# Seven-product downs two steps earlier in an attention and mixture-of-experts kernel, with weight forms, loads and attention pieces moved

## The chip, the cores and the metric

The kernel runs on one core of a Trainium2 chip. The metric is device time in microseconds: the median of the runs of one kernel. The kernel before takes 505.33 us (7 runs, 505.01 to 506.3). The engines are TensorE (PE; its weight loads are listed apart as PEld), VectorE (DVE), ScalarE (ACT), GpSimd (POOL) and SyncE (SP). Each runs its own list of instructions in order; what one needs from another it waits for.

## The reference

```python
def _attn_ref(q, k, v):                       # q, k, v: 8 x 8 x 576 x 64
    k_p = k.reshape(B, H, Sp, pool, D).mean(axis=3)      # pool = 8, Sp = 72
    v_p = v.reshape(B, H, Sp, pool, D).mean(axis=3)
    scores = scale * np.matmul(q, k_p.transpose(0, 1, 3, 2))
    scores = scores - np.max(scores, axis=-1, keepdims=True)
    attn = np.exp(scores)
    attn = attn / (np.sum(attn, axis=-1, keepdims=True) + 1e-09)
    return np.matmul(attn, v_p)

def _moe_ref(x, domain_probs, w1, w2):        # x: 4608 x 512, E = 4, F = 1024
    p = domain_probs / (domain_probs.sum(-1, keepdims=True) + 1e-09)
    for e in range(E):
        h = np.maximum(x @ w1[e], 0.0)
        out += p[:, e:e + 1] * (h @ w2[e])
```

x is the attention's output, its heads side by side, token by token.

## The kernel before

**Chunks and steps.** The 4608 tokens are nine chunks of 512: chunk c below 8 holds the first 512 tokens of batch c, and chunk 8 holds the 64 left-over tokens ("rem") of all eight batches. A step is one pair (chunk c, expert e), numbered s = 4c + e; the loop of L983 runs through them. In step s PE makes the hidden values of (c, e), the "up", and multiplies those of step s - 1 with w2, the "down", so the two are interleaved. Most matmuls take weights of w1 or hidden values as stationary operand.

**Ups.** An up is a product of two-by-two blocks. `up_plain` (L671) makes it with eight block products (32 matmuls of 512 columns). `up_seven` (L731) makes it with seven products (`product`, L654; eight matmuls of 256 columns for each, half of them in each half j of the step), which need sums and differences of blocks: the weight forms S1, S2, S4, S3 of w1 (`combine_w1`, L608) and the forms of x (`forms_of`, L619). Each product's bank in PSUM is copied by ACT (`keep`, L702), added to another one with the ReLU by DVE (`relu_sum`, L707), or put through a ReLU by ACT (L711).

**Downs.** A plain down (`down`, L861) is 32 matmuls of 512 columns, and `merge` adds each result, times its probability, to an accumulator. A seven-product down (`half_of`, L770, and `up_down`, L789) uses seven half products of 256 columns, four matmuls each, twice in a step. It needs forms of the hidden values (`sums_of`, L718: three DVE instructions and a GpSimd one, L728) and of w2 (`combine_w2`, L640: t1, t2, t4 go to w2_t, and the last overwrites a block of w2_bf, so that it must come after the last plain down with that expert). `splits` (L715) says which steps have such a down. Its results are merged by four DVE adds for each half of the step (L766); for expert 0 two of them are a scaling by DVE (L821) and one by ACT.

**What sets the order.** All engines' lists are written out by hand. `point()` and `slot()` (L972 to L981) count places; `placed` names what is emitted at a place, and `slot()` first takes one entry of `forms_due`. A step has 16 places, 8 of them slots. `second_attention` (L530) puts the attention of batch 1 at places 42 to 71, and `attention(c)` (L551) that of batch c + 1 at places 2n + 1 after the start of chunk c, for n of its table, while chunk c's experts run. The pieces: a fold adds the eight rows of a pooled key or value (DVE L198 to L249 for batch 1, L214 to L222 for batch 2, POOL for keys from batch 3); `second_keys` and `second_queries` transpose on PE, `keys` and `queries` by DMA (SP); `scores` runs four matmuls and ACT's exp; `context` multiplies with the values and divides on DVE (L385, L386); `turn` transposes x by DMA (L417). The rem pieces of two batches come in odd chunks (L560 to L564).

**Queues.** Loads are DMAs issued by GpSimd (L950 to L965 for the first ones), in the order w1(1), w1(2), w2(1), w1(3), k1, w2(2), q1, v1, w2(3). They stand in its one list with its arithmetic, so a load that waits for its buffer holds up the sums behind it. `loads_wait` (L243) is a copy of one element by which GpSimd waits for kpT before it issues the next loads. w2_t of experts 2 and 3 is also the home of the raw values of batches 1 and 2. SP issues the transposes by DMA and the stores.

**Which forms where.** Before: w1(0) and w2(0) without their last forms, and w1(2), in step 1; w1(3) in step 2; w1(1) and x of chunk 1 in step 4; w1(0)'s last and w2(2) in step 5; w2(3) in step 6; w2(1) in steps 7 and 8 and w2(0)'s last in step 8, all on DVE. Step 4 starts with the eight pieces of the plain down of (0, 3); the plain up of (1, 0) follows (L1051 to L1055).

Of the kernel before, what the change touches and what calls it, by code (L numbers as in the profile page):

```python
# [18 lines left out]
def kernel(  # L19
# [99 lines left out]
    def load_first_q(half):  # L119
# [5 lines left out]
        )  # L125

    def load_q_rem(b):
        if b % 2 == 0:
            q_rems[b // 2] = qpool.tile([P, H, D], BF16, name="q_rem", bufs=2)
        lo = (b % 2) * REM  # L130
        nc.gpsimd.dma_start(
            out=q_rems[b // 2][lo:lo + REM],
            in_=q[b, :, NT:S, :].rearrange("h p d -> p h d"),
        )
# [107 lines left out]

    def loads_wait(b):  # L243
        nc.gpsimd.tensor_copy(out=mark[:], in_=state[("kpT", b)][0:1, 0, 0:1])

# [284 lines left out]
    def second_attention():  # L530

        lo, hi = halves

        return {
            42: [lambda: fold_keys(1, lo)],
            44: [lambda: fold_keys(1, hi), lambda: load_k(2)],
            48: [second_keys],
            51: [lambda: second_queries(0)],
            52: [lambda: second_queries(1), lambda: load_q(2), lambda: load_q_rem(2)],
            54: [lambda: scores(1, 0)],  # L540
            56: [lambda: scores(1, 1), lambda: fold_values(1, lo)],
            58: [lambda: scores(1, 2), lambda: fold_values(1, hi)],
            60: [lambda: scores(1, 3)],
            61: [lambda: context(1, 0), lambda: turn(1, 0)],
            63: [lambda: context(1, 1), lambda: turn(1, 1)],
            66: [lambda: context(1, 2), lambda: turn(1, 2)],
            69: [lambda: context(1, 3), lambda: turn(1, 3)],
            71: [lambda: load_v(2)],
        }

    def attention(c):  # L551
# [8 lines left out]
        if c % 2:  # L560
            i = c // 2
            q_at = 15 if b < B else 2
            for n, piece in zip((0, 8, 11, 12), (rem_queries, rem_scores, rem_context, rem_turn)):
                add(q_at + n, lambda piece=piece: piece(i))  # L564
# [5 lines left out]
        if c == 1:  # L570
            add(3, lambda: queries(b))
            add(2, *key_parts(b)[:2])
            add(3, *key_parts(b)[2:])
            add(3, lambda: keys(b), lambda: loads_wait(b))
            add(3, lambda: (load_q(b + 1), load_q_rem(b + 1)))
            for pair in range(NPAIR):
                add(8 + pair, lambda pair=pair: scores(b, pair))
            for n, part in enumerate(value_parts(b)):
                add(7 + n, part)
            mixed = (12, 13, 14, 15)  # L580
        else:
# [8 lines left out]
        if more:  # L590
            add(4, lambda: load_half(b + 1, k, "kraw", 0))
            add(11, lambda: queries(b + 1))
            add(8, lambda: load_half(b + 1, k, "kraw", 1))
            add(16, *key_parts(b + 1))
            add(21, lambda: load_half(b + 1, v, "vraw", 0))
            add(27, lambda: load_half(b + 1, v, "vraw", 1))
            add(24, lambda: keys(b + 1))
# [117 lines left out]
    def splits(c, e):  # L715
        return (1, 2) <= (c, e) < (B, E - 1)

# [212 lines left out]
    with tc.manual_schedule(engines={ENG.PE, ENG.DVE, ENG.Activation, ENG.Pool, ENG.SP}):  # L930
# [25 lines left out]
        load_w1(2)  # L956
        load_w2(1)
        load_w1(3)
        load_k(1)
        load_w2(2)  # L960
        load_q(1)
        load_v(1)
# [20 lines left out]
        for s in range(len(steps) + 1):  # L983
# [15 lines left out]

            nothing = [lambda: None] * 4  # L1000
            if s == 1:
                w, u, x = combine_w2(0), combine_w1(0), forms_of(0)
                forms_due.extend([lambda w=w, u=u, n=n: (w[n](), u[n]()) for n in range(3)])
                forms_due.extend(nothing[:1] + combine_w1(2))
                for part in x[:3]:
                    part()
            elif s == 2:
                x[3]()
                forms_due.extend(nothing + combine_w1(3))
            elif s == 4:  # L1010
                x = forms_of(1)
                u1 = combine_w1(1)
                forms_due.extend(nothing + [
                    lambda: (u1[0](), u1[1]()), lambda: (u1[2](), u1[3]()), lambda: x[0](),
                    lambda: (x[1](), x[2]()),
                ])
            elif s == 5:
                x[3]()
                forms_due.extend(u[3:] + nothing[:2] + combine_w2(2))
            elif s == 6:  # L1020
                v3 = combine_w2(3)
                forms_due.extend(nothing[:1] + v3[:1] + nothing[:2] + v3[1:])
            elif s == 7:
                v2 = combine_w2(1)
                forms_due.extend(nothing[:1] + v2[:1] + nothing[:3] + v2[1:2])
            elif s == 8:
                forms_due.extend(nothing[:1] + w[3:] + v2[2:3] + nothing[:2] + v2[3:])
            elif s == E * B + 1:
                reload_w2(E - 1)
            for j in range(2):  # L1030
# [20 lines left out]
                elif s == E:  # L1051
                    for n in range(4):
                        between(j, n)
                    if j:
                        up_plain(c, e, range(FCH))  # L1055
                elif splits(*steps[s - 1]):
                    up_down(c, e, j, *steps[s - 1])
# [32 lines left out]
```

## Time and profile before

| what | us |
|---|---|
| median of the runs | 505.33 |
| the profiled execution, its own time | 505.47 |
| its span, first to last instruction | 503.8 |
| PE busy | 492.5 |
| DVE busy | 354.7 |
| ACT busy | 287.1 |
| POOL busy | 182.4 |

The profile is of one execution. A busy time is the union of an engine's instructions; the span is 1.67 us shorter than the time of the execution. A row of the timeline gives the start, the length, engine, line, operation, what is written and read, how many instructions are merged in it, and in brackets how long the engine sat idle before it and what ended that. Where this text says "from start to start", the gap is counted from one matmul's start to the next, less the usual distance, since a matmul's recorded end overlaps with the next one. A few matmuls are missing from the records. By that count PE lost 9.8 us against full streaming between 17 and 142 us, and 12.7 us in all of the rest up to 500 us, where nearly all of it is the usual distance of 0.109 us between matmuls of 256 columns against 0.107 us of streaming.

### The profile page before, as it was taken

Reading aid. Unit: us, or ns where it says so; the run is one execution under the profiler, and the core shown is the slowest. Engines: PE = TensorE matmul, PEld = TensorE weight load, DVE = VectorE, ACT = ScalarE, POOL = GpSimd, SP = SyncE. Lnnn points to the kernel's source line nnn. Section 1 sums busy time; section 2 is a strip of 40 time slices with the busy share of each in tenths; the row PEclk is TensorE's granted clock in tenths of the full one; section 3 lists DMA queues with packets and bytes.
Section 4 is the critical chain, followed back from the end, with each engine's and each line's share of the span. In section 5 each row is a group of like instructions: output and inputs, shape, how many; then the busy total and the mean of one; then the engine's idle time right before and its main releaser. Section 6 shows DMA issues by size and latency. Waiting matters only on the chain.

```text
span 503.8 us, 10971 instructions
## 1 busy us (share of the span) xinstructions
PE 492.5 (98%) x4485; PEld 392.5 (78%) x4499; DVE 354.7 (70%) x643; ACT 287.1 (57%) x531; POOL 182.4 (36%) x169
## 2 busy tenths in 40 slices
PE   8899899999999999999999999999999999999996
PEld 3746554667788888888788888888888888888884
DVE  1364889667877767777777777767777767776674
ACT  3654444645576567655766576666665565556650
POOL 8463202145423662266126722661115111512110
PEclk9999999999999999999999999999999999999999
DMA  9999999963826364935573286332210110012003
GB/s 123 205 205 205 202 170 175 124 62 47 98 83 98 48 66 113 109 48 60 111 108 59 19 128 110 53 44 60 64 20 13 44 43 12 1 44 64 2 1 83
DMA packets 84754, 41.90 MB, mean 83 GB/s; under 512 B 48720, under 2 KB 80208, under 8 KB 84704
## 3 DMA queue, kind: packets, MB, share of 16 engines
q0 software_dynamic: 43200, 22.91, 35.7%
q1 hardware_dynamic: 41104, 17.77, 17.1%
q8 instruction: 35, 0.57, 0.5%
q10 hardware_dynamic: 400, 0.52, 0.3%
q14 instruction: 15, 0.12, 0.1%
HBM read 45.69 MB, written 9.44 MB: 109 GB/s over the span
## 4 chain that ended last, share of the span: by engine, by line
PE 82%; DMA 9%; DVE 4%; POOL 2%; issue 1%; ACT 1%; POOLq 0%; ACTq 0%
PE g_ps L660 36%; PE u_ps L782 34%; PE o_ps L876 5%; DMA w_bf<-in_moe_w_dram 5%; DMA q_sb<-in_q_dram 3%; PE two L272 2%; PE two L395 1%; PE h_ps L678 1%; DMA H_sb<-in_v_dram 1%; DVE acc L766 1%; DVE H_sb L708 1%; POOL w_bf L146 1%; DVE x_tok L386 1%; DVE w_bf L651 0%; PE o_ps L891 0%
## 5 line engine op out<-in xcount | busy, mean ns | idle before, releaser
L660 PEld LDWEIGHTS <-w_bf 128*128 128x128 bf16 x1848 | 177.8, 98 | 29.3 <-issue 3.2
L766 DVE SCALAR_TENSOR_TENSOR acc<-u_ps,p_all,acc 128x512 f32<-128x512 f32 (+1 forms) x204 | 121.1, 594 | 76.7 <-ACT u_ps L819 72.4
L728 POOL TENSOR_TENSOR h_s<-H_sb,h_s 128x1024 bf16<-128x1024 bf16 x29 | 61.4, 2117 | 232.1 <-DVE h_s L727 232.1
L660 PE MATMUL g_ps<-xT,w_bf 128*128 128x256 bf16 x928 | 129.9, 273 | 0.5 <-DVE H_sb L708 0.5
L660 PE MATMUL g_ps<-xf,w_bf 128*128 128x256 bf16 x792 | 109.8, 272 | 0.7 <-ACT g_ps L803 0.4
L704 ACT COPY r<-g_ps 128x512 f32<-128x512 f32 x140 | 82.0, 586 | 49.8 <-PE g_ps L660 45.2
L708 DVE CUSTOM_DVE_ANT_0 H_sb<-g_ps,r 128x512 bf16<-128x512 f32 x140 | 96.2, 688 | 13.2 <-ACT r L704 8.8
L782 PEld LDWEIGHTS <-H_sb 128*128 128x128 bf16 x928 | 86.7, 98 | 18.2 <-DVE H_sb L726 4.9
L782 PE MATMUL u_ps<-w_bf,H_sb 128*128 128x256 bf16 x696 | 95.3, 273 | 0.4 <-DVE H_sb L726 0.3
L711 ACT ACTIVATE H_sb<-g_ps 128x512 bf16<-128x512 f32 x124 | 74.0, 597 | 20.5 <-PE g_ps L660 20.5
L782 PEld LDWEIGHTS <-h_s 128*128 128x128 bf16 x696 | 68.1, 98 | 7.9
L803 ACT COPY g_ps<-g_ps 128x512 f32<-128x512 f32 x58 | 33.1, 570 | 65.3 <-PE g_ps L660 65.3
L782 PE MATMUL u_ps<-w_t,h_s 128*128 128x256 bf16 x464 | 69.6, 273 | 0.0
L876 PE MATMUL o_ps<-w_bf,H_sb 128*128 128x512 bf16 x205 | 51.3, 379 | 0.7 <-issue 0.2
L819 ACT COPY u_ps<-u_ps 128x256 f32<-128x256 f32 x58 | 20.7, 357 | 32.9 <-PE u_ps L782 32.6
L782 PE MATMUL u_ps<-w_t,H_sb 128*128 128x256 bf16 x232 | 35.0, 273 | 0.0
L782 PE MATMUL u_ps<-w_bf,h_s 128*128 128x256 bf16 x232 | 34.8, 273 | 0.0
L876 PEld LDWEIGHTS <-H_sb 128*128 128x128 bf16 x216 | 20.6, 98 | 18.2 <-issue 0.8
L276 ACT ACTIVATE expT<-two 72x1024 bf16<-72x1024 f32 x28 | 28.5, 1017 | 1.3 <-PE two L272 1.3
L386 DVE TENSOR_TENSOR x_tok<-two,inv 128x512 bf16<-128x512 f32 x32 | 22.1, 691 | 1.1
L821 DVE TENSOR_SCALAR acc<-u_ps,p_all 128x512 f32<-128x512 f32 x14 | 10.5, 750 | 16.5 <-ACT u_ps L819 16.5
L807 ACT COPY u_ps<-u_ps 128x256 f32<-128x256 f32 x58 | 21.1, 363 | 0.0
(119 smaller groups left out, 435.1 us busy)
## 6 DMA issues: line engine op xcount, KB each, us to landing
out_dram<-acc SPq DMA_DIRECT2D x32, 256.0 KB, 2.4
w_bf<-in_moe_w_dram POOLq DMA_DIRECT2D x17, 256.0 KB, 8.9
w_bf<-in_moe_w_dram POOLq DMA_DIRECT2D x8, 512.0 KB, 14.8
q_sb<-in_q_dram POOLq DMA_DIRECT2D x7, 512.0 KB, 10.3
raw_kv<-in_k_dram POOLq DMA_DIRECT2D x10, 288.0 KB, 6.5
raw_kv<-in_v_dram POOLq DMA_DIRECT2D x10, 288.0 KB, 6.1
raw_kv<-in_k_dram POOLq DMA_DIRECT2D x2, 576.0 KB, 15.6
w_t<-in_v_dram POOLq DMA_DIRECT2D x2, 576.0 KB, 13.7
```

The lines of the kernel that those rows point to most:

```text
L276: nc.scalar.activation(out=state[("expT", b)][:, 2 * pair:2 * pair + 2].rearrange("j h r s p -> j s (h r) p"), in_=two[0:SP].rearrange("j ...
L386: nc.vector.tensor_tensor(out=x_tok, in0=c_ps[:, :, :, 0:D], in1=inv[:].unsqueeze(3).to_broadcast([P, 2, NPAIR, D]), op=ALU.mult,)
L660: nc.tensor.matmul(bank[:, t, :], lhsT=w1_bf[:, e, block, kc, lo:lo + P], rhs=x[:, kc, :], start=(first and t == 0 and kc == 0), stop=(t = ...
L704: nc.scalar.copy(out=r[:], in_=ps[:])
L708: nc.vector._custom_dve(TENSOR_ADD_SAT, out=out, in0=ps[:], in1=r[:], s0=BIG, s1=0.0)
L711: nc.scalar.activation(out=out, in_=ps[:], func=ACT.Relu)
L728: lambda: nc.gpsimd.tensor_sub(out=s4, in0=a12, in1=s2),
L766: nc.vector.scalar_tensor_tensor(out=acc, in0=ps, scalar=prob, in1=acc, op0=ALU.mult, op1=ALU.add,)
L782: nc.tensor.matmul(out, lhsT=lhs[0][:, lhs[1] + f, lhs[2]], rhs=rhs[0][:, rhs[1] + f, rhs[2]], start=(start and f == 0), stop=(f == FCH // ...
L803: nc.scalar.copy(out=s[:], in_=g[:])
L807: nc.scalar.copy(out=two[:, lo], in_=one[:, lo])
L876: nc.tensor.matmul(sums[r][:], lhsT=hidden[(c, e)][:, fc, r * P:(r + 1) * P], rhs=w2_bf[:, e, fc, :], start=(fc == 0), stop=(fc == FCH - 1),)
```

## The change

- `splits` begins at (1, 0) instead of (1, 2): the downs of these two steps are made with seven products. The plain up of (1, 0) is followed by the sums of its hidden values.
- The forms they need come earlier: w2(0)'s last in step 1; w1(1)'s in step 2; w2(1)'s all on GpSimd, placed at 60 in step 3, behind a one-element copy that waits for the values of batch 1 and the load of v2 (both from place 71). w1(3)'s are split over the end of step 2 and the start of step 3; w2(2)'s and w2(3)'s go to steps 5 to 8.
- k1 is loaded ahead of w1(3), and q1 in two halves by heads. The folds and transposes of k1 move up by one place, two contexts of batch 1 move back by one.
- The attention of batch 2 in chunk 1 is moved back and spread: queries from n = 3 to 4, folds from 2 and 3 to 6 and 7, keys from 3 to 7, the mark and loads behind it to 8, scores from 8 to 11 to 8, 10, 12, 14, values from 7 to 9, contexts from 12 to 15 to 16, 18, 20, 21; the halves of k3 from 4 and 8 to 8 and 12.
- The rem pieces stand at 0, 9, 13, 14 instead of 0, 8, 11, 12 after their start; in the last chunk they start at 3 instead of 2.

```diff
+    def load_q_halves(b):
+        raws[("q", b)] = qpool.tile([P, H, NR, D], BF16, name="q_sb")
+        for hs in halves:
+            nc.gpsimd.dma_start(
+                out=raws[("q", b)][:, hs].rearrange("p h r d -> p h (r d)"),
+                in_=q[b, hs, 0:NT, :].rearrange("h (p r) d -> p h (r d)", r=NR),
+            )
...
-    def loads_wait(b):
-        nc.gpsimd.tensor_copy(out=mark[:], in_=state[("kpT", b)][0:1, 0, 0:1])
+    def pool_waits(one):
+        nc.gpsimd.tensor_copy(out=mark[:], in_=one)
...
-            42: [lambda: fold_keys(1, lo)],
-            44: [lambda: fold_keys(1, hi), lambda: load_k(2)],
-            48: [second_keys],
+            41: [lambda: fold_keys(1, lo)],
+            43: [lambda: fold_keys(1, hi), lambda: load_k(2)],
+            47: [second_keys],
...
-            63: [lambda: context(1, 1), lambda: turn(1, 1)],
-            66: [lambda: context(1, 2), lambda: turn(1, 2)],
+            64: [lambda: context(1, 1), lambda: turn(1, 1)],
+            67: [lambda: context(1, 2), lambda: turn(1, 2)],
             69: [lambda: context(1, 3), lambda: turn(1, 3)],
-            71: [lambda: load_v(2)],
...
-            q_at = 15 if b < B else 2
-            for n, piece in zip((0, 8, 11, 12), (rem_queries, rem_scores, rem_context, rem_turn)):
+            q_at = 15 if b < B else 3
+            for n, piece in zip((0, 9, 13, 14), (rem_queries, rem_scores, rem_context, rem_turn)):
...
-            add(3, lambda: queries(b))
-            add(2, *key_parts(b)[:2])
-            add(3, *key_parts(b)[2:])
-            add(3, lambda: keys(b), lambda: loads_wait(b))
-            add(3, lambda: (load_q(b + 1), load_q_rem(b + 1)))
+            add(4, lambda: queries(b))
+            add(6, *key_parts(b)[:2])
+            add(7, *key_parts(b)[2:])
+            add(7, lambda: keys(b))
+            add(8, lambda: pool_waits(state[("kpT", b)][0:1, 0, 0:1]))
+            add(8, lambda: (load_q(b + 1), load_q_rem(b + 1)))
             for pair in range(NPAIR):
-                add(8 + pair, lambda pair=pair: scores(b, pair))
+                add(8 + 2 * pair, lambda pair=pair: scores(b, pair))
             for n, part in enumerate(value_parts(b)):
-                add(7 + n, part)
-            mixed = (12, 13, 14, 15)
+                add(9 + n, part)
+            mixed = (16, 18, 20, 21)
...
-            add(4, lambda: load_half(b + 1, k, "kraw", 0))
+            add(8 if c == 1 else 4, lambda: load_half(b + 1, k, "kraw", 0))
...
-            add(8, lambda: load_half(b + 1, k, "kraw", 1))
+            add(12 if c == 1 else 8, lambda: load_half(b + 1, k, "kraw", 1))
...
-        return (1, 2) <= (c, e) < (B, E - 1)
+        return (1, 0) <= (c, e) < (B, E - 1)
...
+        load_k(1)
         load_w1(3)
-        load_k(1)
         load_w2(2)
-        load_q(1)
+        load_q_halves(1)
...
+            if s == 3:
+                placed.setdefault(60, []).extend(
+                    [lambda: pool_waits(vps[1][0:1, H - 1, 0:1]), lambda: load_v(2)]
+                    + combine_w2(1, nc.gpsimd))
...
-                forms_due.extend(nothing[:1] + combine_w1(2))
+                forms_due.extend(w[3:] + combine_w1(2))
...
-                forms_due.extend(nothing + combine_w1(3))
+                u1, v1 = combine_w1(1), combine_w1(3)
+                forms_due.extend([lambda: (u1[0](), u1[1]()), lambda: (u1[2](), u1[3]())]
+                                 + nothing + v1[:2])
+            elif s == 3:
+                forms_due.extend([v1[3], v1[2]])
             elif s == 4:
                 x = forms_of(1)
-                u1 = combine_w1(1)
-                forms_due.extend(nothing + [
-                    lambda: (u1[0](), u1[1]()), lambda: (u1[2](), u1[3]()), lambda: x[0](),
-                    lambda: (x[1](), x[2]()),
+                forms_due.extend(nothing + nothing[:2] + [
+                    lambda: x[0](), lambda: (x[1](), x[2]()),
                 ])
             elif s == 5:
                 x[3]()
-                forms_due.extend(u[3:] + nothing[:2] + combine_w2(2))
+                w2f = combine_w2(2)
+                forms_due.extend(nothing[:3] + u[3:] + w2f[:1] + nothing[:2] + w2f[1:2])
             elif s == 6:
                 v3 = combine_w2(3)
-                forms_due.extend(nothing[:1] + v3[:1] + nothing[:2] + v3[1:])
+                forms_due.extend(nothing[:3] + w2f[2:] + nothing[:2] + v3[:1])
             elif s == 7:
-                v2 = combine_w2(1)
-                forms_due.extend(nothing[:1] + v2[:1] + nothing[:3] + v2[1:2])
-            elif s == 8:
-                forms_due.extend(nothing[:1] + w[3:] + v2[2:3] + nothing[:2] + v2[3:])
+                forms_due.extend(nothing[:3] + v3[3:] + v3[1:2] + nothing[:2] + v3[2:3])
...
                         up_plain(c, e, range(FCH))
+                        for part in sums_of(c, e):
+                            part()
```

## The prediction

> **What bounds the kernel now.** I read the page's table of engines first, then busy time by window, then the timelines of PE, VectorE (DVE) and GpSimd (POOL) up to 160 us, where nearly all that the change touches lies.
>
> ```profile
> PE 492.5 (98%) x4485; PEld 392.5 (78%) x4499; DVE 354.7 (70%) x643; ACT 287.1 (57%) x531; POOL 182.4 (36%) x169
> PEclk9999999999999999999999999999999999999999
> ```
>
> TensorE is busy for 98% of 503.8 us and its clock is granted in full in every slice. So the time falls only by work taken off PE, or by its few pauses. By step (the columns are the window, its length, busy us of PE, of weight loads, DVE, ACT, POOL, the granted clock, DMA share and GB/s; steps 5, 6, 7 and an undisturbed late one):
>
> ```profile
> 86.30:102.60 16.30, 15.99 (x136) 9.83 (x137) 11.18 (x24) 11.24 (x17) 3.30 (x4) 1.00 0.98 108
> 102.60:116.10 13.50, 13.40 (x105) 8.86 (x105) 9.85 (x15) 5.07 (x9) 6.11 (x7) 1.00 0.62 68
> 116.10:129.30 13.20, 12.96 (x131) 11.21 (x129) 9.89 (x19) 7.62 (x15) 10.04 (x8) 1.00 0.31 31
> 381.50:393.90 12.40, 12.40 (x115) 10.94 (x113) 9.00 (x16) 7.06 (x15) 6.65 (x5) 1.00 0.01 1
> ```
>
> The late row is the price of a step whose down is split: 112 matmuls of 256 columns in 12.3 us, 0.109 us each. In step 3 the pauses stand together:
>
> ```profile
> 53.16 1.03 PE L660 MATMUL g_ps<-xT,w_bf 128*128 128x256 bf16 x8 [0.48 <-DVE H_sb L708]
> 54.74 0.30 PE L320 MATMUL kpt_ps<-ident,kp 72*128 72x72 bf16 x4 [0.42 <-DVE kp L207]
> 57.75 0.62 PE L330 MATMUL qt_ps<-ident,q_sb 128*128 128x128 bf16 x8 [0.32 <-DMA q_sb<-in_q_dram]
> 59.15 0.61 PE L330 MATMUL qt_ps<-ident,q_sb 128*128 128x128 bf16 x8
> ...
> 72.64 0.43 PE L395 MATMUL two<-vp,expT 72*128 72x65 bf16 x8 [0.34 <-DVE x_tok L386]
> ```
>
> The first two have one cause on DVE: its fold of k1 waited for the load, and the ReLU sum behind it (L708) came late:
>
> ```profile
> 50.23 0.69 DVE L198 TENSOR_TENSOR raw_kv<-raw_kv 72x1024 bf16<-72x1024 bf16 x1 [1.28 <-DMA raw_kv<-in_k_dram]
> ```
>
> **The change part by part.**
>
> *Seven-product downs of steps (1,0) and (1,1).* A plain down is 32 matmuls of 512 columns; 31 recorded ones spread over 32 places take 26.11 to 33.0 us, 0.216 each, so 6.91 us. Seven half products are 56 of 256 columns at 0.109, 6.12 us. Twice 0.80: **-1.6 us** of pure PE work.
>
> *k1 ahead of w1(3); folds one slot earlier; w1(1) forms earlier.* The loads run at 205 GB/s and land in order; a quarter of w1 lands 1.28 us after the one before it, k1 4.05 us after. Swapped, k1 lands near 45.1 instead of 50.2, and w1(3) at 50.2. DVE reaches the first fold at 47.5 (end of L708 that starts at 46.87), so it waits for nothing; both folds (1.7 us each, from L198 to L207) and the ReLU sum between them end at 51.5, the sum that PE needs at 52.1, before PE's 52.5. Both pauses go, 0.65 + 0.58 from start to start. The w1(3) form is then reached at about 52.7, 2.5 us after its landing. The third pause is limited by q1, whose bytes come at the same place: its first half should land 1.3 us ahead of 57.7 (half of 512 KB, by the quarters of w1). PE, from 52.5 with the k1 transposes (0.25), two products (0.87), three down matmuls (0.65), two products (0.87) and four downs (0.86), gets to the first transposes at 56.0, waits 0.4, and does the second ones at 57.8 instead of 59.15: **-1.35 us**. The w1(1) forms (four of 0.60 us, starts of rows 28.71 and 29.31) sit in step 2 where DVE was busy 8.2 of 13.7 us, and w2(0)'s last in a 3.6 us idle stretch of DVE before 36.0: nothing; without that cover they would cost a sum of 0.6 each ahead of L708.
>
> *Step 4.* Contexts move by a slot; the wait at 72.64 stays, one place on. x of chunk 1 is needed by L678, which started at 79.43 when the last transpose had landed at 79.0, 2.7 us after its issue. PE now comes at 78.0, while the loads ahead of the transposes end where they did (v2 at 76.6). Bounds 0 and 0.8, taken **+0.3**.
>
> *Steps 5 and 6 under the new form.* The sums of hidden (1,0) can start only after the last ReLU of L682, 0.8 us after PE ends step 4's up; half 1 needs that ReLU too, at 0.45: +0.35. DVE's queue for step 5, start to start: sums 1.9, x form 0.4, per half of the step 0.67 + 2 x 0.60 + 2 x 0.40 (5.3 together), value folds 2.8, w1(0)'s last form 0.6, two w2(2) forms 1.2, next sums 1.9: 14.1 us, against PE's 12.2 + 1.4 for four scores. DVE is therefore full; after the ReLU sum of low, done at 5.5 us into the step (0.7 behind product 7's copy), stand 0.4 + 1.4 (fold) + 0.4, so the sum that ends the first half is done at 8.3 where product 5 of the second half asks at 7.9: +0.45. Before, step 5 lost 0.37 at a context. Step 6: contexts 3.4, three w2(2) forms 1.8, 6.7 of merges and ReLU sums, sums 1.9, so 13.8 against 13.3: +0.1. Together **+0.5** (bounds 0 and 2).
>
> *w2(1) on GpSimd.* Four subtractions of 128x1024 at 2.12 us (L728's mean): 8.5 us, after v2's issue, so 67.3 to 75.8. What stands behind them there is the sum of (1,0), due at 88. DVE in that time has only instructions with a PSUM operand. It takes four forms of w2(1) from DVE in steps 7 and 8, and w2(0)'s. A rule speaks against it:
>
> ```profile
> 109.86 1.74 POOL L222 TENSOR_TENSOR kp<-raw_kv 72x256 bf16<-72x256 bf16 x2
> ...
> 110.10 0.98 DVE L649 TENSOR_TENSOR w_t<-w_bf,w_t 128x1024 bf16<-128x1024 bf16 x1
> ```
>
> The DVE form took 0.98 instead of 0.68 beside a POOL instruction of 0.67. The Trainium skill (SBUF — State Buffer, "SBUF: two separate sides") says why: the two share a port pair under an exclusive lock, and a DVE instruction with two SBUF inputs waits for the whole of a GpSimd one. By the row the loss is 0.3, inside slack, nothing. By the rule it is up to 2.1. The forms of w2(1) miss it; but two w2(3) forms now stand just behind the sums, one merge (0.67) after POOL starts its 2.12 us sum, so each would be held 1.45, and PE would feel some 0.45 of it at product 3. I take the rule's side: **+0.9** in steps 7 and 8. The pauses there before (0.41, 0.44, 0.27 from start to start) go with the lighter queue: **-1.0**; a late sum at the start of step 7 gives back **+0.3**.
>
> *Attention 2 a step later; GpSimd's queue.* The mark now waits for kpT(2) behind the sum of (1,0), so q3, its rest and the first half of k3 are issued near 92.5 instead of 87.4 (the columns: start, length):
>
> ```profile
> 94.86 1.41 POOL L95 DMA_DIRECT2D raw_kv<-in_k_dram  x1 [6.67 <-DMA raw_kv<-in_k_dram]
> 106.15 1.15 POOL L219 TENSOR_TENSOR raw_kv<-raw_kv 72x512 bf16<-72x512 bf16 x1 [9.89 <-DMA raw_kv<-in_k_dram]
> ```
>
> The halves took 7.2 and 11.2 us to land. Half 1 can be issued at 99.9, and the sum of (1,1) stands behind it on POOL, ready on DVE at 101.7, wanted by half 3 at 105.7: 1.8 us of slack. Half 1 lands between 107.8 (6.5, the median) and 112.5; then POOL's folds (4.9), a load issue, the sum of (1,2) 2.1: done 117.6 to 120.5, wanted at 119.1. **+0.3** (0 to 1.4). Chunk 2's x forms follow on POOL by 125.2, wanted near 126.5.
>
> *Rem pieces spread.* Rem scores a slot later, context two: late chunks paused 0.345 us at 223.6 and 328.9 (on ACT's copy, L803, behind the exp) and 0.26 at 420.1. In a scores slot the exp stands behind the copy that matters: **-0.7** (0 to -0.95).
>
> Sum: -1.6 - 1.35 + 0.3 + 0.5 + 0.9 - 1.0 + 0.3 + 0.3 - 0.7 = -2.35. The profiled execution took 505.47 (span 503.8); that becomes 503.1, and with the median 0.14 lower 503.0. The added items are the guesses and the removed ones mostly rows, so I lean by 0.3 to the better: **502.7 us**.
>
> **Rivals.**
> - *Pauses nearly all vanish (0.25).* If the lock and DVE's full queue cost nothing: -1.6 - 1.35 - 1.0 - 0.95 - 0.37 + 0.35 = -4.9, near 500.7 with a little left over. For it: steady chunks run at 12.3 us with DVE at 9.0. Against it: 14.1 us of DVE in 13.6.
> - *DVE becomes the bound in steps 5 to 8 (0.17).* Each form behind the sums costs its 1.45 and step 5 its full surplus: +2 more, 504.7, no change that can be told.
> - *GpSimd's queue becomes the bound (0.13): slower.* If the first half of k3 also takes 11.2 us, as the second did beside transposes, the sum of (1,1) ends at 107.4, 1.7 late; the second half then lands at 116.5, its folds end at 121.4, and the sum of (1,2) at 124.4 against 120.8: 3.6. Together +5.3 - 0.3: 507.7. It decides from a first half over about 10 us. Against it: nothing but q3 moves in the DMA engines when it is issued.
> - My forecast has 0.45.
>
> **How the numbers follow.** A difference of 0.2%, 1.0 us, is about what can be told: faster means below 504.3. Forecast and first rival are faster (0.70), and a third of the second (0.05); the rest of it is "same" (0.10) or slower (0.02). Slower: that and the third rival, 0.15. Faster 0.75, same 0.10, slower 0.15. The range leaves out the third rival and the far end of the first: 500.6 to 505.2.
>
> **What would show it.** PE's pauses at 53 and 54 us gone, and the second q1 transposes near 57.8; steps 5 and 6 together near 27.8 us instead of 29.8 (86.3 to 116.1); POOL's four w2(1) rows of 2.1 us before 77; w2(3) forms of over 1 us on DVE after the sums if the lock is real. Wrong: a wait of DVE on w1(3) near 52 us, PE waiting for GpSimd's sum in steps 6 and 7, or a start of step 8 later than 127.2 (before 129.3).

## The result, and the profile after

The changed kernel takes 503.84 us (median; 502.49 to 504.65), the kernel before 505.53 on the same chips. The ratio is 0.9963, with a 95% interval of 0.9954 to 0.9971: faster, by 0.37%. The forecast was 502.7 with a range of 500.6 to 505.2. The profiled execution took 503.18, its span is 501.5 at a full clock; the one before took 505.47 with 503.8.

Line numbers from L208 on are about 8 higher than before: the gate products L660 are now L668, the down halves L782 are L790, the merges L766 are L774, the ReLU sum L708 is L716, the weight forms L648 to L651 are L656 to L659, the plain down L876 is L884.

The page's table of engines, after:

```profile
PE 491.0 (98%) x4537; PEld 397.8 (79%) x4547; DVE 361.8 (72%) x651; ACT 290.0 (58%) x541; POOL 196.0 (39%) x177
```

TensorE's busy time falls by 1.5 us (492.5 before). (The 9.8 us lost between 17 and 142 us, named ahead of the prediction, count eight unrecorded matmuls as pauses; with these taken as run it is 8.0, and 7.0 after.) Busy time by window (the window, its length, then PE, weight loads, DVE, ACT, POOL, clock, DMA share and GB/s) for steps 5, 6 and 7 after:

```profile
85.30:99.80 14.50, 14.29 (x129) 11.06 (x128) 11.13 (x22) 11.50 (x20) 4.69 (x6) 1.00 0.56 66
99.80:113.10 13.30, 13.30 (x147) 11.98 (x145) 12.66 (x25) 7.59 (x16) 7.81 (x7) 1.00 0.84 102
113.10:127.50 14.40, 13.57 (x147) 11.46 (x145) 14.30 (x22) 7.90 (x15) 12.29 (x11) 1.00 0.41 49
```

Steps 5 and 6 take 27.85 us from first matmul to first matmul instead of 29.74. Step 6 has no idle time on PE at all. But step 7 has become longer, 14.38 us instead of 13.18: PE is idle for 0.83 of it, and DVE is busy for 14.30 of 14.40. Only part of the 1.2 us is work that moved in (PE's busy time 13.57 instead of 12.95).

In step 3, PE's timeline (start, length, operation, idle time before it) has none of the pauses that the prediction showed at 53 and 54 us, and one of 0.36 from start to start (57.90 to 58.26, 0.26 over a matmul's own time) ahead of the second half of the q1 transposes:

```profile
53.16 0.42 PE L328 MATMUL kpt_ps<-ident,kp 72*128 72x72 bf16 x8
53.42 1.04 PE L668 MATMUL g_ps<-xT,w_bf 128*128 128x256 bf16 x8
...
56.69 0.61 PE L338 MATMUL qt_ps<-ident,q_sb 128*128 128x128 bf16 x8
57.13 0.60 PE L668 MATMUL g_ps<-xf,w_bf 128*128 128x256 bf16 x4
57.57 0.60 PE L668 MATMUL g_ps<-xT,w_bf 128*128 128x256 bf16 x4
58.26 0.62 PE L338 MATMUL qt_ps<-ident,q_sb 128*128 128x128 bf16 x8
```

The lost time of step 7 stands on DVE's timeline. The two w2(3) forms (L656 here, L658 in step 8) come behind the sums of a hidden block, and while GpSimd runs its own part of those sums they take 2.24 us instead of 0.68:

```profile
115.27 0.68 DVE L735 TENSOR_TENSOR h_s<-h_s,H_sb 128x1024 bf16<-128x1024 bf16 x1
115.87 0.75 DVE L774 SCALAR_TENSOR_TENSOR acc<-u_ps,p_all,acc 128x512 f32<-128x512 f32 x1
116.53 2.24 DVE L656 TENSOR_TENSOR w_t<-w_bf 128x1024 bf16<-128x1024 bf16 x1
118.69 0.74 DVE L774 SCALAR_TENSOR_TENSOR acc<-u_ps,p_all,acc 128x512 f32<-128x512 f32 x1
...
130.51 2.23 DVE L658 TENSOR_TENSOR w_t<-w_bf,w_t 128x1024 bf16<-128x1024 bf16 x1
```

GpSimd's timeline has the other side; its sum ends at 118.21, and the form ends 0.56 after that:

```profile
116.10 2.11 POOL L736 TENSOR_TENSOR h_s<-H_sb,h_s 128x1024 bf16<-128x1024 bf16 x1 [1.23 <-DVE h_s L735]
```

And PE's timeline has who pays: a down half that needs the merge behind the form.

```profile
119.48 0.60 PE L790 MATMUL u_ps<-w_t,H_sb 128*128 128x256 bf16 x4 [0.83 <-DVE acc L774]
...
133.46 0.60 PE L790 MATMUL u_ps<-w_t,H_sb 128*128 128x256 bf16 x4 [0.50 <-DVE acc L774]
```

From start to start these are 0.99 and 0.67 us over a matmul's own time, and behind each comes one more of 0.165 for the ReLU sum: 2.0 us in all (0.1 of the 0.67 stands behind four scores at the other places too).

### The profile page after: what moved, and what is told of

Same layout as the page of the kernel before. It is cut to its first block, busy times and chain, and to the rows that moved or that the text cites. A ratio compares the mean times of both kernels' runs of the same rounds, so it can differ in the third digit from the quotient of the medians.

```text
span 501.5 us, 11093 instructions
## 1 busy us (share of the span) xinstructions
PE 491.0 (98%) x4537; PEld 397.8 (79%) x4547; DVE 361.8 (72%) x651; ACT 290.0 (58%) x541; POOL 196.0 (39%) x177
## 4 chain that ended last, share of the span: by engine, by line
PE 82%; DMA 9%; DVE 4%; POOL 2%; issue 1%; ACT 1%; POOLq 0%; ACTq 0%
PE u_ps L790 37%; PE g_ps L668 37%; PE o_ps L884 3%; DMA raw_kv<-in_k_dram 3%; DMA w_bf<-in_moe_w_dram 3%; DMA q_sb<-in_q_dram 3%; PE two L280 2%; PE two L403 1%; PE h_ps L686 1%; DMA H_sb<-in_v_dram 1%; DVE acc L774 1%; POOL w_bf L154 1%; DVE H_sb L716 1%; DVE w_t L658 0%; DVE w_t L656 0%
## 5 line engine op out<-in xcount | busy, mean ns | idle before, releaser
L668 PEld LDWEIGHTS <-w_bf 128*128 128x128 bf16 x1848 | 178.7, 98 | 26.4 <-issue 1.3
L774 DVE SCALAR_TENSOR_TENSOR acc<-u_ps,p_all,acc 128x512 f32<-128x512 f32 (+1 forms) x216 | 127.6, 592 | 70.1 <-ACT u_ps L827 65.9
L736 POOL TENSOR_TENSOR h_s<-H_sb,h_s 128x1024 bf16<-128x1024 bf16 x31 | 66.0, 2128 | 240.5 <-DVE h_s L735 228.1
L668 PE MATMUL g_ps<-xT,w_bf 128*128 128x256 bf16 x928 | 129.9, 273 | 0.0
L668 PE MATMUL g_ps<-xf,w_bf 128*128 128x256 bf16 x792 | 109.3, 272 | 0.6 <-DVE H_sb L716 0.2
L790 PEld LDWEIGHTS <-H_sb 128*128 128x128 bf16 x992 | 92.5, 98 | 20.1 <-issue 6.0
L790 PE MATMUL u_ps<-w_bf,H_sb 128*128 128x256 bf16 x744 | 102.0, 273 | 0.0
L716 DVE CUSTOM_DVE_ANT_0 H_sb<-g_ps,r 128x512 bf16<-128x512 f32 x136 | 93.5, 688 | 2.8 <-ACT r L712 2.5
L790 PEld LDWEIGHTS <-h_s 128*128 128x128 bf16 x744 | 72.8, 98 | 8.4
L811 ACT COPY g_ps<-g_ps 128x512 f32<-128x512 f32 x62 | 35.4, 570 | 73.5 <-PE g_ps L668 73.5
L790 PE MATMUL u_ps<-w_t,h_s 128*128 128x256 bf16 x496 | 74.4, 273 | 0.0
L827 ACT COPY u_ps<-u_ps 128x256 f32<-128x256 f32 x62 | 22.2, 358 | 34.1 <-PE u_ps L790 33.7
L790 PE MATMUL u_ps<-w_t,H_sb 128*128 128x256 bf16 x248 | 37.3, 273 | 1.3 <-DVE acc L774 1.3
L790 PE MATMUL u_ps<-w_bf,h_s 128*128 128x256 bf16 x248 | 37.2, 273 | 0.0
L884 PE MATMUL o_ps<-w_bf,H_sb 128*128 128x512 bf16 x145 | 35.6, 379 | 0.5 <-issue 0.2
L884 PEld LDWEIGHTS <-H_sb 128*128 128x128 bf16 x152 | 14.3, 98 | 14.1 <-issue 0.8
L733 DVE TENSOR_TENSOR h_s<-H_sb 128x1024 bf16<-128x1024 bf16 x31 | 21.1, 682 | 2.7 <-ACT H_sb L690 2.7
```

Source lines behind the costliest of these rows:

```text
L668: nc.tensor.matmul(bank[:, t, :], lhsT=w1_bf[:, e, block, kc, lo:lo + P], rhs=x[:, kc, :], start=(first and t == 0 and kc == 0), stop=(t = ...
L716: nc.vector._custom_dve(TENSOR_ADD_SAT, out=out, in0=ps[:], in1=r[:], s0=BIG, s1=0.0)
L736: lambda: nc.gpsimd.tensor_sub(out=s4, in0=a12, in1=s2),
L774: nc.vector.scalar_tensor_tensor(out=acc, in0=ps, scalar=prob, in1=acc, op0=ALU.mult, op1=ALU.add,)
L790: nc.tensor.matmul(out, lhsT=lhs[0][:, lhs[1] + f, lhs[2]], rhs=rhs[0][:, rhs[1] + f, rhs[2]], start=(start and f == 0), stop=(f == FCH // ...
L811: nc.scalar.copy(out=s[:], in_=g[:])
```

## The experiments

A number that recurs below is the time from the start of step 4's plain up (L678 before, L686 after) to the start of the last plain down, in the profiled execution. Ahead of that up the loads set the pace: an execution that begins early waits there for x. Of the six variants of the change below whose first down began at 25.3 to 26.3 us, five waited, by 0.4 to 2.5 us, while the change's profiled execution (26.77) did not. Three other ones began their first down only at 27.8 to 28.0: TensorE's granted clock was 0.50 in them from 16.5 to 19.6 us, and 1.00 in the change. So the stretch behind that up compares kernels better than the span. It is 413.16 us before and 411.87 after.

**Are the two held forms what the change loses?** Three edits treat them in three ways. The lock's theory says that a form beside GpSimd's sum is held until that ends; its rival says that DVE's queue is full in step 7, so that taking away the overlap changes nothing.

*The forms away from the sums:*

```diff
-                forms_due.extend(nothing[:3] + w2f[2:] + nothing[:2] + v3[:1])
+                forms_due.extend(nothing[:3] + w2f[2:] + nothing[:1] + v3[:1])
...
-                forms_due.extend(nothing[:3] + v3[3:] + v3[1:2] + nothing[:2] + v3[2:3])
+                forms_due.extend(nothing[:4] + v3[3:] + v3[1:2] + v3[2:3])
```

> The changed kernel, with the two w2(3) forms that stand one merge behind the sums of (1,2) and (1,3) moved one place ahead (before those sums), and the last block form beside them moved one place back. The number of DVE instructions in steps 6 to 8 stays. Lock theory (each form is held while GpSimd makes its 2.12 us sum): both forms take 0.68 to 1.1 us instead of 2.24, PE's pauses of 0.99 + 0.17 and 0.67 + 0.17 at half 4 of steps 7 and 8 go, about 2.0 us less than the changed kernel: span near 499.5, median near 501.9. Queue theory (DVE has too much to do in these steps, wherever a form stands): pauses of the same sum stay, elsewhere in the steps; median 503.3 to 504.0.

It took 503.36 (502.74 to 504.38), a ratio of 0.996 (0.9948 to 0.9973) to the kernel before: no different from the change, where the lock's theory wanted 501.9. The pauses at the old place are gone, and others took their place. DVE's timeline, then PE's:

```profile
112.71 1.04 DVE L656 TENSOR_TENSOR w_t<-w_bf 128x1024 bf16<-128x1024 bf16 x1
113.68 0.47 DVE L774 SCALAR_TENSOR_TENSOR acc<-u_ps,p_all,acc 128x256 f32<-128x256 f32 x1
114.07 0.68 DVE L716 CUSTOM_DVE_ANT_0 H_sb<-g_ps,r 128x512 bf16<-128x512 f32 x1
```

```profile
114.80 0.38 PE L668 MATMUL g_ps<-xf,w_bf 128*128 128x256 bf16 x2 [0.82 <-DVE H_sb L716]
```

The form now stands ahead of the ReLU sum that PE needs (and beside GpSimd's folds of k, which stretch it to 1.04). In step 8 the same happens twice, with forms of 0.68 that nothing holds: pauses of 0.78 at 127.90 and 0.44 at 129.56 (here and below a pause is named by the start of the matmul ahead of it). So the time alone seems to be for the rival, but the trace is not: a slot that holds nothing up was not found by counting slots.

*The sums of (1,2) and (1,3) all on DVE:*

```diff
+        fourth = nc.vector if (c, e) in ((1, 2), (1, 3)) else nc.gpsimd
...
-            lambda: nc.gpsimd.tensor_sub(out=s4, in0=a12, in1=s2),
+            lambda: fourth.tensor_sub(out=s4, in0=a12, in1=s2),
```

> The changed kernel, with the fourth sum of hidden (1,2) and of (1,3) on DVE instead of GpSimd; the two w2(3) forms stay where they are. DVE gets 0.6 us more in each of steps 7 and 8, and GpSimd holds nothing when the forms come. Lock theory: the forms take 0.68 us, the merge behind them starts 0.9 us earlier than in the changed kernel, so PE's pauses of 0.99 and 0.67 at half 4 shrink to 0 to 0.2: about 1.5 us less, median near 502.3. Queue theory: the pauses grow by about 0.6 each, median near 505.

It took 503.02 (502.56 to 503.58; 0.9952, 0.9939 to 0.9966). In step 8 the form takes 0.68 and PE's pause is gone. In step 7 GpSimd, free of the sum, went on to its x forms (1.34 us, then two in 3.04), and these stretched DVE's sum (1.45) and the form (0.98): a pause of 1.30 in place of 0.99. That is a mixed result: one pause of the two obeys, and the time lies between the 502.3 and 505 that the two theories wanted.

*The forms directly behind DVE's own sums, ahead of the merge.* A list is emptied between the sums and the merge in the function that interleaves an up with a down:

```diff
+        while behind_sums:
+            behind_sums.pop()()
...
-                forms_due.extend(nothing[:3] + w2f[2:] + nothing[:2] + v3[:1])
+                forms_due.extend(nothing[:3] + w2f[2:])
...
-                forms_due.extend(nothing[:3] + v3[3:] + v3[1:2] + nothing[:2] + v3[2:3])
+                forms_due.extend(nothing[:3] + v3[3:] + v3[1:2])
...
+                    if j and s in (6, 7):
+                        behind_sums.append(v3[0] if s == 6 else v3[2])
```

> The changed kernel, with the two w2(3) forms that stood one merge behind the sums of (1,2) and (1,3) put directly behind the third sum, ahead of that merge, where DVE can begin before GpSimd has its semaphore. DVE's work in steps 6 to 8 is the same and nothing comes ahead of a ReLU sum that PE waits for. Lock theory: both forms take 0.7 us instead of 2.24, GpSimd's sum starts 0.6 later, PE's pauses at half 4 (0.99 + 0.17, 0.67 + 0.17) go to 0 to 0.2 each: from the start of step 4's up to the end of the span 2.0 us less than the changed kernel's 423.06, median near 502.0. Queue theory (the run with the forms ahead of the sums only moved the pauses because the work is too much): half of it or more stays, median 503 or over.

It took **501.40** (500.37 to 502.28; ratio 0.9915, 0.9899 to 0.9930), better than both kernels. DVE's timeline, then GpSimd's (line numbers are one higher here; L775 is the merge):

```profile
116.18 0.69 DVE L736 TENSOR_TENSOR h_s<-h_s,H_sb 128x1024 bf16<-128x1024 bf16 x1
116.78 0.68 DVE L656 TENSOR_TENSOR w_t<-w_bf 128x1024 bf16<-128x1024 bf16 x1
117.38 1.62 DVE L775 SCALAR_TENSOR_TENSOR acc<-u_ps,p_all,acc 128x512 f32<-128x512 f32 x2
...
129.62 0.68 DVE L658 TENSOR_TENSOR w_t<-w_bf,w_t 128x1024 bf16<-128x1024 bf16 x1
```

```profile
117.02 2.43 POOL L737 TENSOR_TENSOR h_s<-H_sb,h_s 128x1024 bf16<-128x1024 bf16 x1 [1.22 <-DVE h_s L736]
```

The same instruction, one place earlier in DVE's queue, starts 0.24 us before GpSimd's sum and takes its plain 0.68; GpSimd's sum takes 2.43 instead of 2.11. Both pauses of PE are gone, and step 7 is idle nowhere:

```profile
114.00:127.50 13.50, 13.50 (x149) 11.72 (x147) 13.19 (x22) 7.90 (x15) 12.12 (x11) 1.00 0.44 56
```

From step 4's up to the last plain down it takes 410.09 instead of 411.87: 1.78 of the 2.0 us.

**The hold by itself.** The kernel before gets one more subtraction of 128x512 on DVE in each of 18 undisturbed steps, whose result nothing uses: once behind the sums, once a slot earlier, ahead of them.

```diff
+            elif 10 <= s < 28:
+                forms_due.extend(nothing + nothing[:3] + [lambda: nc.vector.tensor_sub(
+                    out=x_rem[:, :, 3 * P:NT], in0=w2_t[:, 0, 0, :, 0:P], in1=w2_t[:, 0, 1, :, 0:P])])
```

(nothing[:2] in place of nothing[:3] is the earlier slot.)

> The kernel before the change, with one more DVE subtraction (two SBUF inputs, 512 elements, into a region of x_rem that is not yet in use) in each of the steps 10 to 27, in the last place, that is behind the sums and the merge that follows them. In 14 of the 18 steps a merge stands between the sums and it, so GpSimd's 2.12 us sum has begun; in the other 4 it follows the sums at once and can begin ahead of GpSimd. Lock theory: in 14 steps it takes 1.9 to 2.2 us instead of 0.42, and PE loses 0.7 to 1.2 in each: 10 to 16 us more, 515 to 521. No lock: 0.42 us of DVE time in steps with over 3 us of idle DVE time, 505.5 to 506.

> The same added subtraction as in the run with it behind the sums, in the same 18 steps, one place earlier, ahead of the sums and of the last ReLU sum, where GpSimd is idle or at work on x forms and folds. Lock theory: 0.42 us each in most steps, up to 1.5 us where GpSimd folds k, and PE loses under 1 us in all: 505.5 to 506.5. If the position does not matter, the same time as the other run.

Behind the sums 513.85 (513.49 to 514.52; 1.0161, 1.0148 to 1.0175), ahead of them 507.63 (506.38 to 508.08; 1.0032, 1.0022 to 1.0043). That one instruction's line in each trace (shortest, median and longest in ns):

```profile
L1031 DVE TENSOR_TENSOR x_rem<-w_t x18: 418/1972/1981, 173.4 to 403.9; 128x512 bf16<-128x512 bf16 x18
```

```profile
L1031 DVE TENSOR_TENSOR x_rem<-w_t x18: 415/416/416, 168.1 to 392.7; 128x512 bf16<-128x512 bf16 x18
```

In the first of the two, 14 of the 18 take 1.97 us. Each of these starts 0.42 to 0.43 us behind the start of GpSimd's sum and ends 0.28 to 0.30 us behind its end. The other four start 0.22 to 0.25 us ahead of that sum and take 0.42. DVE's, GpSimd's and PE's timelines at the first one:

```profile
173.35 1.98 DVE L1031 TENSOR_TENSOR x_rem<-w_t 128x512 bf16<-128x512 bf16 x1
172.93 2.11 POOL L728 TENSOR_TENSOR h_s<-H_sb,h_s 128x1024 bf16<-128x1024 bf16 x1 [4.70 <-DVE h_s L727]
176.04 0.60 PE L782 MATMUL u_ps<-w_t,H_sb 128*128 128x256 bf16 x4 [0.58 <-DVE acc L766]
```

The same work costs 1.97 us or 0.42 by its place, 1.56 us apart, and 6.2 us of the kernel's time, 0.44 for each of the 14. This settles that the hold is real and that it reaches PE. Both times miss what was expected: 513.85 is under 515 to 521, since PE lost less for each hold, and 507.63 is over 505.5 to 506.5, since an instruction that nothing holds still puts the sums behind it off, and PE waits some 0.23 us for them in most of these steps.

**What the other parts are worth.** *Plain downs kept in steps 5 and 6* (with them, no sums behind step 4's up, and the last forms of w2(0) and w2(1) in step 8 again):

```diff
-        return (1, 0) <= (c, e) < (B, E - 1)
+        return (1, 2) <= (c, e) < (B, E - 1)
...
-                        for part in sums_of(c, e):
-                            part()
```

> The changed kernel with plain downs for steps (1,0) and (1,1), as before; the last forms of w2(0) and w2(1), which overwrite what a plain down reads, go to step 8 on DVE; loads, attention and the other forms stay as changed. My prediction's ledger: 1.6 us of PE work comes back, and the 0.35 and 0.38 us pauses in step 5 go, so steps 5 and 6 take some 1 us longer than the changed kernel's 27.85 and the median is near 504.9. Rival (attention 2 spread out is what shortened these steps, and the products are worth nothing net): steps 5 and 6 stay within 0.4 us of 27.85 and the median of 503.84.

It took 503.61 (503.50 to 504.41; 0.9967, 0.9955 to 0.9980): no different from the change (0.9963), so the products, as made, are worth nothing that the medians show; behind the up it takes 412.42, 0.55 more. Each theory was right in one half: the median is the rival's, but steps 5 and 6 take 29.51 us, 1.66 more than in the change. The trace says where the gain went. From step 4's up to the first rem scores in step 7 it takes 38.58 us instead of 36.62, so seven products save 1.96 there. By the scores of batch 3 in step 8 only 0.81 of that is left (54.95 against 54.14), since without the products the first of the two forms stands clear of the sums (0.68 at 113.99) and its 1.15 us of pauses do not arise. Of these 0.81 the stretch up to the last plain down keeps 0.55; three pauses of the change that the next section names take more than the difference.

*The order of the loads as before, and q1 in one piece alone:*

```diff
-        load_k(1)
         load_w1(3)
+        load_k(1)
         load_w2(2)
-        load_q_halves(1)
+        load_q(1)
```

> The changed kernel with w1(3) ahead of k1 again and q1 in one transfer. DVE's first fold stands one place earlier than before and would wait for k1 from 47.5 to about 50.2 or 50.7; w1(3)'s forms stand behind it. My theory: the ReLU sums behind the folds come 2.5 us later, the pauses near 53 us come back, and q1 as a whole stops PE at the first transposes; the transposes of the second half of q1 start 1.0 to 1.6 us later than in the changed kernel, median near 505.2. Rival (DMA time sets step 3 in both orders and the transposes into x hide it): under 0.4 us, median near 504.

> The changed kernel with q1 in one transfer, k1 still ahead of w1(3). PE comes to the first transposes of q1 near 56.7 and would wait for the whole of q1, near 58.0 to 58.2, where the changed kernel waits 0.26 at the second ones. My theory: the second transposes start 0.9 us later (two products behind the first ones), 0.5 to 0.9 us more in all, median near 504.5. Rival (the transposes of x of chunk 1, which land behind v2, give the time back in step 4): under 0.3.

With both undone 504.67 (503.97 to 506.47; 0.9989, 0.9981 to 0.9998), with q1's halves alone undone 504.04 (503.27 to 508.27; 0.9980, 0.9968 to 0.9992). PE's timeline with both undone has the pauses of step 3 again, the first two on the fold of k1 and the ReLU sum behind it, the third on a w1(3) form:

```profile
53.59 0.30 PE L328 MATMUL kpt_ps<-ident,kp 72*128 72x72 bf16 x4 [0.50 <-DVE kp L215]
54.19 1.03 PE L668 MATMUL g_ps<-xT,w_bf 128*128 128x256 bf16 x8 [0.29 <-DVE H_sb L716]
56.71 0.61 PE L668 MATMUL g_ps<-xf,w_bf 128*128 128x256 bf16 x4 [0.40 <-DVE w_bf L622]
59.70 0.61 PE L338 MATMUL qt_ps<-ident,q_sb 128*128 128x128 bf16 x8 [0.20 <-DVE qT L342]
```

Behind step 4's up these two take 411.91 and 411.88 us, what the change takes (411.87), so what the order and the halves are worth lies ahead of that up. Together it is 0.8 us by the medians (1.4 was expected), and 1.75 in the profiled executions (from the first down to that up 53.40 us with both undone, 51.65 in the change). The halves alone are within the spread.

*The rem pieces at their old slots:*

```diff
-            q_at = 15 if b < B else 3
-            for n, piece in zip((0, 9, 13, 14), (rem_queries, rem_scores, rem_context, rem_turn)):
+            q_at = 15 if b < B else 2
+            for n, piece in zip((0, 8, 11, 12), (rem_queries, rem_scores, rem_context, rem_turn)):
```

> The changed kernel with the rem pieces at their old places (0, 8, 11, 12, and 2 in the last chunk). My prediction took 0.7 us for their move, three pauses of 0.345, 0.345 and 0.26: then 0.7 us more, median near 504.5. Rival, by the trace of the changed kernel, in which three new pauses of 0.28 on ACT's copy stand at other places: 0 to 0.3, median 503.8 to 504.1.

It took 504.28 (503.58 to 504.40; 0.9968, 0.9956 to 0.9980), 412.85 behind the up, so the spreading is worth 1.0 us there (0.4 by the medians, within the spread). The pauses of 0.346, 0.345 and 0.26 us are back, at 222.02, 327.53 and 418.70, and step 7 has new ones of 0.35 and 0.48, against 0.7 less at the first held form.

*w2(1) on DVE, in its idle time before step 5:*

```diff
-                    + combine_w2(1, nc.gpsimd))
+)
...
+                placed.setdefault(79, []).extend(combine_w2(1))
```

> The changed kernel with the four w2(1) forms on DVE, at the end of step 4, in its idle 2.7 us ahead of the sums of (1,0), instead of on GpSimd. My prediction costed them at nothing on GpSimd, hidden in its idle time; on DVE they end at about 85.9 where the sums are wanted at 86.1: within 0.3 us of the changed kernel. Rival (they run into the sums): step 5 starts its half 7 late, 0.3 to 1 us more.

It took 503.59 (502.68 to 505.12; 0.9962, 0.9948 to 0.9977), and behind the up 411.95. Which engine makes these four forms does not matter here.

**Further from the better version.** The values' parts one slot earlier, for the pause at product 5 of step 5, and in a second kernel v2's load behind the w2(1) forms on GpSimd as well:

```diff
-                add(9 + n, part)
+                add(8 + n, part)
```

```diff
-                    [lambda: pool_waits(vps[1][0:1, H - 1, 0:1]), lambda: load_v(2)]
-                    + combine_w2(1, nc.gpsimd))
+                    [lambda: pool_waits(vps[1][0:1, H - 1, 0:1])]
+                    + combine_w2(1, nc.gpsimd) + [lambda: load_v(2)])
```

> As the run with the forms directly behind the sums, and the four value pieces of batch 2 one place earlier in step 5, so that the first fold (0.68) falls in DVE's idle 1.0 us ahead of its first merge. The pause of 0.38 at product 5 of step 5's second half should go, since the ReLU sum before it comes 0.7 earlier: 0.3 to 0.4 us less than that run. Rival (GpSimd's sum of (1,0) starts 0.6 later behind the fold and half 3 waits for it): the same or 0.3 more.

> As the run before it in this list, and the load of v2 behind the four w2(1) forms on GpSimd, so that it is issued near 75 instead of 66.7 and its 3 us of DMA time come after the transposes of x of chunk 1. If loads set the start of step 4's up (it began between 78.2 and 78.7 in five runs, whether PE's first down began at 25.7 or 26.8), it begins 0.3 to 0.8 earlier, near 77.8, and the value folds of step 5 still find v2 (landing near 80, wanted near 88). Rival (x itself is as late as that): no change.

The first took 501.35 (500.64 to 504.53; 0.9922, 0.9901 to 0.9944): the pause fell from 0.385 to 0.265, and the time did not change measurably (0.3 to 0.4 us less was expected). Its profiled execution is the slowest of the six, 504.53. It waited 2.35 us for x ahead of step 4's up, and then TensorE's granted clock was 0.50 from 80.8 to 84.1, with matmuls of 512 columns 0.426 us apart instead of 0.216: behind the up 411.70 us, against 410.09 without the earlier values. The second took 509.61 (508.41 to 511.46; 1.0070, 1.0054 to 1.0085), where a gain was looked for. PE waits 6.4 us ahead of step 4's up:

```profile
85.80 1.01 PE L686 MATMUL h_ps<-xT,w_bf 128*128 128x512 bf16 x2 [6.21 <-DMA xT<-x_tok]
```

The load of v2 was issued at 76.25 and the last transpose of x at 76.68, and both landed at 85.66, 9.0 us after the transpose's issue, instead of 2.7 in the change (75.62 to 78.28). Behind this wait the clock is 0.50 for longer (the columns as in the windows above), and the stretch behind the up takes 412.77, another 2.7 us:

```profile
85.80:91.40 5.60, 5.60 (x14) 1.97 (x15) 4.84 (x12) 1.48 (x3) 0.00 (x0) 0.50 0.48 143
```

## Why the prediction was right, point by point

The profiled spans differ by 2.30 us. From the first down on they differ by 2.96, since the change's execution began its first down 0.66 later (v landed at 12.27 instead of 11.86, ahead of anything that the change touches). The 2.96 are -1.55 up to the second q1 transposes, -0.13 to step 4's up, -1.89 in the rest of step 4, step 5 and step 6, +1.20 in step 7, -0.42 to the scores of batch 3, and -0.18 in the 358 us behind them. By the medians the gain is smaller, 1.7; the change's profiled execution is 0.66 under its median.

- *Seven-product downs, -1.6.* Right as PE's work, though not by the busy totals: these are 491.0 with the products and 490.8 in the run without them. That run took 1.96 us longer up to the rem scores, of which its pauses of 0.63 and 0.33, against one of 0.38 in the change, make 0.6; 1.4 is left. It also shows that little of the 1.96 was kept, mostly because of the lock, below.
- *k1 and q1, -1.35.* Right: -1.55 from the first down on. k1 landed at 44.6 (forecast 45.1), w1(3) at 49.8 (50.2), the second q1 transposes began at 58.26 (57.8; less the late start, 57.6). By the medians it is worth 0.8; that an execution which gets ahead waits for x at step 4 is the likely reason, and not shown.
- *Step 4's x, +0.3.* None in this execution; 0.4 to 2.5 in variants that began sooner.
- *Steps 5 and 6, 27.8 us.* Right: 27.85, with a pause of 0.38 at product 5 of the second half (forecast 0.45). Of the 0.35 for the last ReLU only 0.09 came (at 86.17).
- **The lock on two w2(3) forms, +0.9: the term that was mis-sized.** It measured **2.0**. The hold itself was right (forecast 1.45, measured 1.56), and so were the two instructions and the side taken: the Trainium skill's rule (SBUF — State Buffer, "SBUF: two separate sides"), under which a DVE instruction with two SBUF inputs waits for the whole of a GpSimd one, is what the 2.24, 1.97 and 0.42 us show: the held ones end some 0.3 to 0.6 us after GpSimd's. What failed is "PE would feel some 0.45 of it at product 3". Behind the form stands a merge, and a down half needs it before product 3 comes up; it felt 0.99 and 0.67, and the ReLU sum behind that another 0.165 twice. The hold should have been followed to the next instruction on DVE that frees a PSUM buffer.
- *The old pauses of steps 7 and 8, -1.0.* Right: those of 0.41, 0.44, 0.21 and 0.27 are gone.
- *A late sum at step 7's start and GpSimd's queue, +0.3 each.* Neither came. The first half of k3 was issued at 92.45 and landed at 99.43, the second at 99.73 and 108.83 (within the 107.8 to 112.5 given); the sum of (1,2) ended at 118.21, at the early end of 117.6 to 120.5, and PE never waited for a sum of GpSimd's.
- *Rem, -0.7.* Right in sign, 1.0 in size by its experiment.
- *Not in the sum:* three new pauses of 0.285 us, at 156.6, 234.6 and 466.7, on ACT's copy (L811). They are in every variant of the change but the one with plain downs. The trace shows how steps 5 and 6 reach that far. These three copies start 0.36 us after the product that releases them, the other 58 behind 80 us 0.08, and two ReLUs at 311.13 and 388.95 start 0.18 to 0.20 late instead of 0.02. Counted in ACT's list, waits included, the five are the 192nd, 320th, 448th, 576th and 704th entries, 128 apart. The change has ten ACT instructions more than the kernel before (541, 531), which brings these places onto copies that PE waits for; with plain downs (531) no pause follows. What ACT waits for at every 128th entry no run here tells.

So costs of 0.3 that did not come, and a larger gain from rem, stand against the lock's further 1.1 and 0.86 that was not seen. The time of 503.84 is 1.1 above the number given, inside its range; that it came so near is in part luck, since these errors have opposite signs.

The rivals: "pauses nearly all vanish" (500.7) fell with the lock, and the version with the forms ahead of the merge, at 501.4, comes near it. "DVE becomes the bound" (504.7) holds for step 7, where DVE is busy 14.30 of 14.40, but 1.56 of that is waiting in the held form, and the gain is kept elsewhere. "GpSimd's queue" needed a first half of k3 of over 10 us; it took 7.0. A sign that was named for "wrong", a start of step 8 later than 127.2, did appear (127.55). Less the late start of the first down it is 126.9, and 1.15 of it is what the lock cost in step 7. The other signs fell as they should: the four w2(1) rows on GpSimd end at 76.2, and DVE does not wait for w1(3) near 52.

## What to carry to other kernels

When VectorE and GpSimd both work on operands in SBUF, price an added instruction by its place in the queue: find the other engine's long instructions, put it where it starts ahead of one, and look at which buffer the next instruction releases, since that is where the matrix engine feels it. An instruction that nothing holds is not free either: 18 of 0.42 us cost 2.1 us here. Work taken off the busiest engine is worth only what the next wait leaves of it; measure the part alone before crediting it. And where loads set the time of one point, compare kernels from that point on.

## What was not expected of the hardware

An instruction that starts 0.24 us before GpSimd's is not held at all, and GpSimd's own then takes 2.43 us instead of 2.11; started 0.43 us after it, it takes 2.24 instead of 0.68. The same section of the Trainium skill states this too (the order of issue decides who blocks); the prediction used only the half of it that speaks of VectorE waiting, and so did not see that one place earlier in the queue the form would not be held.

A load and a DMA transpose issued 0.43 us apart landed together, 9.4 and 9.0 us later. In the change the same transpose, issued 0.16 us before v2 had landed, took 2.7. Which of the two holds the other, and by what, no run here tells.

A wait of TensorE can cost more than its length. After 2.35 us without a matmul ahead of step 4's up the granted clock was 0.50 for 3.3 us, and after 6.21 us for 6.6; waits of 0.2 to 1.0 us at the same place, in four other variants, left it at 1.00. Where between 1.0 and 2.35 us the limit lies was not measured.
